# Attention with a squared-ReLU MLP: tiles on multiples of 128 bytes, another order of kinds in a pair's second half, and four small steps one step later

## The chip, the cores and the metric

One core of one Trainium2 chip. The metric is the device time of one execution in microseconds; a kernel is timed in several runs and the median is taken. Engines: TensorE (PE in the rows, its weight loads PEld), VectorE (DVE), ScalarE (ACT), GpSimd (POOL), and SyncE (SP), which issues nearly all DMAs here.

## The reference

```
q_pool = q.reshape(B, H, S//2, 2, D).mean(axis=3)      # B=4, H=8, S=1152, D=64: 576 pooled queries
scores = q_pool @ k^T / sqrt(D);  scores -= max(scores)
attn = exp(scores);  attn /= sum(attn) + 1e-9
x = (attn @ v) laid out as 2304 tokens x 512
out = (s * relu(x @ w_in)**2 + b) @ w_out               # 512 -> 2048 -> 512
```

## The kernel before

The program has two stages. Attention runs over 32 heads, two by two: 16 pairs. The MLP follows in three sweeps over 9 token blocks of 256, with features 0 to 2, 3 to 8 and 9 to 15 of 16.

**Attention, step by step.** A head's 1152 keys are 9 blocks of 128, and a step `n` does one block, so a pair has 18 steps, here called step 0 to 17 of the pair (n % 18). In step `n` TensorE computes the scores of block `n` (tile `s`, four matmuls, L497), one or two maximum units for a later pair (tile `m`, L465, each followed by a reduction into `pm` on VectorE), and the value products of block `n - 3` (tile `o`). The order of these parts within a step is the table `ORD`. The order of every other engine's instructions is that in which the code is written: `later(k, f)` puts `f` at the end of the k-th step counted from the present one, and the tables `PREP`, `VS` and `XT` say at which step of a pair a preparation is issued. No scheduler moves anything after that.

**Kinds.** The scores of a block are exponentiated in one of three ways, by the table `KIND` with 18 letters:

- `w`: ScalarE writes one float32 tile `pe`; the value product is four float32 matmuls (L529).
- `v`: ScalarE writes the rounded `ph`, then the full value back into PSUM over `s`; VectorE writes the remainder `pl` = `s` - `ph` (L512); the value product is six matmuls (L535, L537, L539). `s` is free only when `pl` is written.
- `g`: as `v`, but the full value goes to `pe` and GpSimd writes `pl`.

There are two `s` tiles. The scores of step n therefore wait for whatever frees the `s` tile of step n - 2: ScalarE for `w` and `g`, VectorE's `pl` for `v`. `pl(12)` below is the remainder of step 12.

**What else stands in a pair's steps.** `ka`, `kb` and `qt` transpose the next keys and queries on VectorE (`kT`, `kT`, `qT`); `qh`, `qz`, `kl`, `ql` and the roundings `kh` run on GpSimd, `qm` on ScalarE. `prep_v` rounds the next head's values on GpSimd (`vv`, and `vl` behind it at the step's end), from `vf`, which SyncE is told to load four steps earlier. When a head's last value product is done (`finish`), ScalarE copies it to `xu`, VectorE transposes the sums (`invert`, tile `lt`), takes reciprocals and spreads them (`rr`), and GpSimd scales (`xo`). `XT` holds the five delays of these. The first of them puts `invert` at the end of step 11 for head one of a pair, and at the end of the next pair's step 2 for head two.

**Where tiles lie.** The pools put tiles one behind the other in each partition, in order of the code. `sb`, of 8 bytes, stands ahead of nearly all of them, `guard` (8 bytes) ahead of `kraw`, `c` (20 bytes) ahead of `vf`. In the built program the first sweep's weights, `xr` and `x` begin 32 bytes past a multiple of 128, and so do `kraw`, `qraw`, `kT`, `qT`, `kh` and `qh`; `vf`, `vv`, `vl`, `pe`, `ph` and `pl` begin 96 bytes past one; `kk`, `qq`, `qz`, `gh`, `gl`, the raw weights and the later sweeps' weights begin at multiples of 256.

Of the kernel before, what the change touches and what calls it, by code (L numbers as in the profile page):

```python
# [8 lines left out]
F32 = mybir.dt.float32  # L9
F32R = mybir.dt.float32r  # L10
# [21 lines left out]
KB = 384  # L32


KIND = "wvwvgvwvg" + "vwgvvwvgw"

PP = (("ka", 0), ("kb", 0), ("ha", 0), ("hb", 1), ("qs", 1), ("qt", 1), ("qm", 2), ("qh", 2), ("qz", 2), ("kl", 2), ("ql", 3), ("l0", 7))
PREP = (("qs", 9), ("ka", 10), ("kb", 11), ("ha", 11), ("qt", 12), ("hb", 12), ("kl", 12), ("qm", 13), ("qh", 13), ("qz", 13), ("ql", 14), ("l0", 4), ("l1", 13))
LR = 14
LD = 1  # L40
VS = (7, 16)
XT = (1, 2, 3, 4, 8)
SW = (3, 9)
CB, CP = 270, 18
WB = (7, 11)
# [7 lines left out]
def f32(ap):  # L53
    return ap.bitcast(F32)
# [3 lines left out]
def attention_moe_kernel(ctx: ExitStack, tc: tile.TileContext, q, k, v, w_in, w_out, s_in, b_in, out):  # L58
# [6 lines left out]
    P = 128  # L65
    NJ = S // P
    NB = S // 32
    NBQ = SQ // 32
    NT4 = SQ // P
# [10 lines left out]
    consts = ctx.enter_context(tc.tile_pool(name="consts", bufs=1))  # L80
# [2 lines left out]
    mox = ctx.enter_context(tc.tile_pool(name="mox", bufs=1))  # L83
    ep = ctx.enter_context(tc.tile_pool(name="ep", bufs=1))

    sb = consts.tile([P, 2], F32, name="sb")
    xd = [dram.tile([NC, P, SQ], F32, name=f"xd{b}") for b in range(B)]
    parts = {}
    ready = {}
# [131 lines left out]
    def later(k, fn):  # L221
        step[1] += 1
        queue.append((step[0] + k, step[1], fn))
# [97 lines left out]
    ap = att.enter_context(tc.tile_pool(name="ap", bufs=1))  # L321
# [8 lines left out]
    qm = ap.tile([P, P], F32R, name="qm")  # L330
# [2 lines left out]
    vfs = [late.tile([P, NJ, P], F32, name=f"vf{i}") for i in range(2)]  # L333
    vvs = [late.tile([P, NJ, P], F32R, name=f"vv{i}") for i in range(2)]
    vls = [late.tile([P, NJ, D if i == 0 else P], F32R, name=f"vl{i}") for i in range(2)]
    guard = ap.tile([P, 2], F32, name="guard")

    def side(hd, of="v"):

        h = hd % 2 if of == "v" else 1 - hd % 2  # L340
        return slice(h * D, (h + 1) * D)
# [17 lines left out]
    def load_q(p):  # L359
        qraw[p] = ap.tile([P, NBQ, 2, 32], F32, tag="qraw", name=f"qraw{p}")  # L360
        for r, b, h, c in quarters(p):
            for e in range(2):

                eng = nc.sync if p or (r.start == P - 32) else nc.scalar
                eng.dma_start(qraw[p][r, :, e], q[b, h, e::2, c].rearrange("(j t) i -> t j i", t=32))
# [3 lines left out]
    def load_v(hd):  # L369
        nc.sync.dma_start(vfs[hd % 2][:, :, side(hd)], v[hd // H, hd % H].rearrange("(j p) d -> p j d", p=P))  # L370
# [62 lines left out]
    def prep_v(hd):  # L433
        vf, vv, vl = vfs[hd % 2][:, :, side(hd)], vvs[hd % 2][:, :, side(hd)], vls[hd % 2]
        if hd % 2:
            vl = vl[:, :, side(hd)]
        hi_of(nc.gpsimd, vv, vf)

        def lo():
            nc.gpsimd.tensor_tensor(out=vl, in0=vf, in1=f32(vv), op=ALU.subtract)  # L440
            holds["v", hd % 2] = hd

        later(1, lo)
# [27 lines left out]
    def shift(hd, pm, full, rest):  # L471


        c = ap.tile([P, NT4 + 1], F32R, tag="c", bufs=2, name=f"c{hd}")
        row = qqs[hd % 3][:, 1].rearrange("p a n -> p (a n)")
        h = hd % 2
        nc.vector.tensor_reduce(out=c, in_=pm, axis=AX.X, op=ALU.max)

        eng = nc.scalar if hd < 3 else nc.sync

        def send():
            eng.dma_start(f32(row[D:D + 1, :NT4 * P]), f32(c[:, full]))
            eng.dma_start(f32(row[D:D + 1, NT4 * P:]), f32(c[h * D:(h + 1) * D, rest:rest + 1]))
            holds["c", hd % 3] = hd

        later(1, send)
# [4 lines left out]
    def score_step(hd, j, kind):  # L491
        assert holds["k", hd % 3] == holds["c", hd % 3] == hd
        kk, qq = kks[hd % 3], qqs[hd % 3]
        ps = ps_s.tile([P, 2, 512], F32, tag="s", name=f"s{hd}_{j}")
        for a in range(2):
            for i in range(2):
                nc.tensor.matmul(ps[:, a, :HALF], kk[:, i, j * P:(j + 1) * P], qq[:, i, a], start=(i == 0), stop=(i == 1))  # L497
        if kind != "v":
            pe = late.tile([P, 2, HALF], F32, tag="pe", bufs=PE, name=f"pe{hd}_{j}")
        if kind == "w":  # L500
            nc.scalar.activation(pe, ps[:, :, :HALF], AF.Exp, scale=SCALE)
            prob[hd, j] = pe, None
            return
        ph = late.tile([P, 2, HALF], F32R, tag="ph", bufs=PB, name=f"ph{hd}_{j}")
        pl = late.tile([P, 2, HALF], F32R, tag="pl", bufs=PB, name=f"pl{hd}_{j}")
        nc.scalar.activation(ph, ps[:, :, :HALF], AF.Exp, scale=SCALE)  # L506

        full = ps[:, :, :HALF] if kind == "v" else pe
        nc.scalar.activation(full, ps[:, :, :HALF], AF.Exp, scale=SCALE)  # L509
        prob[hd, j] = ph, pl  # L510
        eng = nc.vector if kind == "v" else nc.gpsimd
        fresh.append(lambda: eng.tensor_tensor(out=pl, in0=full, in1=f32(ph), op=ALU.subtract))  # L512
# [3 lines left out]
    inv = {}  # L516
# [27 lines left out]
    def finish(hd, a):  # L544
        p, h = divmod(hd, 2)
        if a == 0:
            xu[hd] = ep.tile([P, 2, HALF], F32, tag=f"xu{h}", name=f"xu{hd}")
        nc.scalar.activation(xu[hd][:, a], acc[hd][a][:, :HALF], AF.Identity, bias=guard[:, h:h + 1])
        if a == 0:
            return  # L550
        acc.pop(hd)
        x = xu[hd].rearrange("p a n -> p (a n)")

        def invert():
            if h == 0:
                inv[p] = ep.tile([P, NBQ, 32], F32, tag="lt", name=f"lt{p}")
            nc.vector.transpose(out=inv[p][side(hd)], in_=x[side(hd, "l")])  # L557

        def reciprocal():
            lt = inv[p]  # L560
            rc = inv[p] = ep.tile([P, NBQ, 1], F32, tag="rc", name=f"rc{p}")
            nc.vector.reciprocal(rc, lt[:, :, 0:1])

        def spread():
            rc = inv[p]
            inv[p] = ep.tile([P, NBQ, 32], F32, tag="lt", name=f"rr{p}")
            nc.vector.transpose(out=inv[p], in_=rc.to_broadcast([P, NBQ, 32]))

        def scale():
            xo = xs[p] = ep.tile([P, SQ], F32, tag="xo", name=f"xo{p}")  # L570
            rr = inv.pop(p).rearrange("p j c -> p (j c)")
            for i in (hd - 1, hd):
                r = side(i)
                nc.gpsimd.tensor_tensor(out=xo[r], in0=xu.pop(i)[r].rearrange("p a n -> p (a n)"), in1=rr[r], op=ALU.mult)

        def send():
            nc.sync.dma_start(xd[hd // H][(hd % H) // 2], xs.pop(p))

        if h == 0:
            later(XT[0], invert)  # L580
        else:
            for at, fn in zip(XT, (invert, reciprocal, spread, scale, send)):
                later(at, fn)
# [53 lines left out]
    for n in range(NS + LAG):  # L637
        hd, j = divmod(n, NJ)
# [4 lines left out]
        for part in ORD[at] if at is not None else "sff":  # L643
            if part == "s" and n < NS:
                score_step(hd, j, KIND[n % 18])
            elif part == "f":
# [10 lines left out]
        if n < NS:  # L657
            p, h = divmod(hd, 2)
# [3 lines left out]
            if n == LD:  # L662
                load_k(2)
                load_q(2)
            if n % 18 == PREP[0][1]:
                lays = {k: prep[k] for k in ("l0", "l1") if k in prep}
                prep = prep_pair(p + 2) if p + 2 < NPAIR else {}
            for name, at in PREP:

                ops = prep if name not in ("l0", "l1") or at < PREP[0][1] else lays  # L670
                if n % 18 == at and name in ops and n >= 8:
# [5 lines left out]
            if hd + 1 < NH:  # L677
                if j == LAG and hd >= 1:
                    load_v(hd + 1)
                if n % 18 in VS:  # L680
                    prep_v(hd + 1)
# [36 lines left out]
    for m in range(len(work) + DEPTH):  # L718
        if m < len(work):
            i, blk, f, fs = work[m]  # L720
# [10 lines left out]
        if m >= DEPTH:  # L731
            _, blk, f, fs = work[m - DEPTH]
# [35 lines left out]
```

## Time and profile before

| | us |
|---|---|
| median of 3 runs | 957.25 (955.07 to 959.66) |
| the profiled execution's own time | 954.59 |
| its span, first to last instruction | 952.8 |
| attention's steps, first score to last score | 24.4 to 533.4 |
| an ordinary pair | 30.9 to 31.0 |

The profiled execution lies 2.66 below the median of the runs, and 1.8 of its time is outside the span. In the profile's rows a time stands in us from the span's start; "idle before <- X" is how long the engine had nothing to do before an instruction and what ended that. A matmul's row begins when it starts to stream and its end is modelled, so that rows of TensorE overlap by some 0.15 us, and the first of the matmuls behind a float32 one shows some 0.2 us early. Ends of whole groups are compared for that reason.

### The profile page before, as it was taken

The numbers are of one execution on the slowest core, as the hardware profiler recorded it, in microseconds if no ns is written. First come the engines' busy times: TensorE is split into PE (matmuls) and PEld (weight loads), VectorE is DVE, ScalarE is ACT, GpSimd is POOL, SyncE is SP. The second block draws the span as 40 slices with busy tenths as digits, with TensorE's granted clock in tenths as the row PEclk, the third lists the DMA queues.
The fourth block names the chain that finished last, engine by engine and source line by source line (L and its number), as shares of the span: only waits on it lengthen the run. The fifth ranks groups of instructions, "written<-read, shape, count | busy, mean of one in ns | idle before, by whom it ended". The sixth has DMA issues, their size and how long they took to land.

```text
span 952.8 us, 16142 instructions
## 1 busy us (share of the span) xinstructions
PE 910.5 (96%) x5712; PEld 818.7 (86%) x5712; DVE 639.7 (67%) x1184; ACT 525.3 (55%) x990; POOL 530.1 (56%) x426
## 2 busy tenths in 40 slices
PE   3799999999999999999999999999999999999998
PEld 2688998889898888888888878889999899999997
DVE  4777777787778778988886477766667653333333
ACT  2566666666666666766677556654444343333332
POOL 6567676867686668778867577754544521111110
PEclk9799999999999999999999999999999999999999
DMA  9888989798977998897754155654354332223211
GB/s 146 135 158 159 157 157 148 148 147 168 140 161 144 186 144 167 157 185 140 172 140 104 60 165 197 220 189 156 111 165 146 133 111 67 75 82 111 67 45 45
DMA packets 255313, 131.18 MB, mean 138 GB/s; under 512 B 203776, under 2 KB 227328, under 8 KB 255232
## 3 DMA queue, kind: packets, MB, share of 16 engines
q1 hardware_dynamic: 251008, 129.69, 61.7%
q10 hardware_dynamic: 4224, 0.45, 0.5%
q8 instruction: 46, 0.75, 0.3%
q14 instruction: 35, 0.29, 0.1%
HBM read 68.68 MB, written 18.87 MB: 92 GB/s over the span
## 4 chain that ended last, share of the span: by engine, by line
PE 68%; DVE 11%; DMA 5%; POOL 5%; ACT 3%; issue 3%; SPq 2%; ACTq 0%; POOLq 0%; DVEq 0%
PE h L272 17%; PE y L299 17%; PE s L497 11%; PE o L529 6%; PE m L465 6%; PE o L539 4%; PE o L535 4%; PE o L537 4%; DVE pm L466 3%; DVE pl L512 2%; POOL pl L512 1%; DVE lt L557 1%; DVE kT L420 1%; DMA yd_True<-yo_True_False 1%; DMA xr<-xd 1%
## 5 line engine op out<-in xcount | busy, mean ns | idle before, releaser
L466 DVE TENSOR_REDUCE pm<-m 128x1 f32<-128x384 f32 x432 | 227.1, 546 | 77.6 <-PE m L465 76.3
L497 PE MATMUL s<-qq,kk 128*128 128x288 f32 x1152 | 222.4, 315 | 10.5 <-DVE pl L512 9.3
L272 PE MATMUL h<-x,wih 128*128 128x256 f32 x1152 | 213.6, 283 | 4.3 <-DVE gl L286 3.5
L497 PEld LDWEIGHTS s<-qq,kk 128*128 128x128 f32 x1152 | 174.7, 190 | 32.8 <-PE m L465 17.4
L272 PEld LDWEIGHTS h<-x,wih 128*128 128x128 f32 x1152 | 185.8, 189 | 19.7 <-DVE gl L286 4.7
L506 ACT ACTIVATE ph<-s 128x576 fp32r<-128x576 f32 x192 | 125.2, 652 | 75.9 <-PE s L497 72.2
L272 PE MATMUL h<-x,wil 128*128 128x256 f32 x576 | 162.2, 282 | 0.0
L512 POOL TENSOR_TENSOR pl<-pe,ph 128x576 fp32r<-128x576 f32 x64 | 91.4, 1427 | 107.8 <-ACT pe L509 101.4
L280 DVE SCALAR_TENSOR_TENSOR h<-h,sb,r 128x256 f32<-128x256 f32 x144 | 70.3, 488 | 114.9 <-ACT r L289 114.9
L253 POOL TENSOR_TENSOR x<-xr,x 128x1024 fp32r<-128x1024 f32 x27 | 65.1, 2410 | 146.3 <-ACT x L212 140.6
L465 PE MATMUL m<-kh,qz 128*128 128x384 f32 x384 | 142.7, 383 | 1.5 <-DVE pm L466 0.9
L529 PE MATMUL o<-pe,vf 128*128 128x288 f32 x384 | 119.4, 408 | 0.0
L539 PE MATMUL o<-pl,vv 128*128 128x288 f32 x384 | 113.8, 296 | 4.6 <-POOL pl L512 4.6
L289 ACT ACTIVATE r<-h 128x256 f32<-128x256 f32 x144 | 55.7, 387 | 111.8 <-PE h L272 111.7
L512 DVE TENSOR_TENSOR pl<-s,ph 128x576 fp32r<-128x576 f32 x128 | 96.2, 751 | 27.3 <-ACT s L509 25.4
L535 PE MATMUL o<-ph,vv 128*128 128x288 f32 x384 | 114.2, 297 | 0.0
L537 PE MATMUL o<-ph,vl 128*64 128x288 f32 (+1 forms) x384 | 113.3, 295 | 0.0
L299 PE MATMUL y<-wol,gh 128*128 128x512 f32 x288 | 113.1, 393 | 0.0
L299 PE MATMUL y<-woh,gl 128*128 128x512 f32 x288 | 113.0, 392 | 0.0
L299 PE MATMUL y<-woh,gh 128*128 128x512 f32 x288 | 112.7, 391 | 0.0
L272 PEld LDWEIGHTS h<-x,wil 128*128 128x128 f32 x576 | 109.6, 190 | 0.0
L283 ACT ACTIVATE gh<-h,sb 128x256 fp32r<-128x256 f32 x144 | 68.4, 475 | 64.5 <-DVE h L280 64.0
(91 smaller groups left out, 1528.0 us busy)
## 6 DMA issues: line engine op xcount, KB each, us to landing
kk<-kh SPq DMA_DIRECT2D x32, 576.0 KB, 6.3
kraw<-in_k_dram SPq DMA_DIRECT2D x64, 144.0 KB, 4.4
vf<-in_v_dram SPq DMA_DIRECT2D x32, 288.0 KB, 4.3
kk<-kT SPq DMA_DIRECT2D x32, 288.0 KB, 3.9
qq<-qh SPq DMA_DIRECT2D x64, 144.0 KB, 5.6
xr<-xd SPq DMA_DIRECT2D x18, 512.0 KB, 3.9
qraw<-in_q_dram SPq DMA_DIRECT2D x122, 72.0 KB, 3.7
wsti<-in_moe_w_in_dram SPq DMA_DIRECT2D x16, 512.0 KB, 4.5
```

The source lines that it names most:

```text
L272: nc.tensor.matmul(h[:, :TB], st[:, c, :], mv[:, c, :], start=(n == 0), stop=(n == 3 * NC - 1))
L280: nc.vector.scalar_tensor_tensor(out=t, in0=h[:, :TB], scalar=sb[:, 0:1], in1=r, op0=ALU.mult, op1=ALU.mult)
L299: nc.tensor.matmul(y[:, :DM], st[:, ts_], mv, start=(first and n == 0), stop=(last and n == 2))
L465: nc.tensor.matmul(ps[:, :KB], st, khs[p][:, e * KB:(e + 1) * KB], start=True, stop=True)
L466: nc.vector.tensor_reduce(out=pms[p][:, col, e:e + 1], in_=ps[:, :KB], axis=AX.X, op=ALU.max)
L497: nc.tensor.matmul(ps[:, a, :HALF], kk[:, i, j * P:(j + 1) * P], qq[:, i, a], start=(i == 0), stop=(i == 1))
L506: nc.scalar.activation(ph, ps[:, :, :HALF], AF.Exp, scale=SCALE)
L512: fresh.append(lambda: eng.tensor_tensor(out=pl, in0=full, in1=f32(ph), op=ALU.subtract))
L529: nc.tensor.matmul(o[:, :HALF], vfs[hd % 2][:, j], ph[:, a], start=first, stop=last)
L535: nc.tensor.matmul(o[:, :HALF], vv[:, j], ph[:, a], start=first, stop=False)
L537: nc.tensor.matmul(o[0:vl.shape[2], :HALF], vl[:, j], ph[:, a], start=False, stop=False)
L539: nc.tensor.matmul(o[:, :HALF], vv[:, j], pl[:, a], start=False, stop=last)
```

## The change

The sizes of three small tiles become 128 bytes, and `guard` moves into `sb`. No instruction is added or removed. In the built program `sb` still begins at a multiple of 128, and now every tile behind it does too: the first sweep's weights, `xr`, `x` and `xu` at multiples of 256; `kraw`, `qraw`, `kT`, `qT`, `kh`, `qh`, `kk`, `qq`, `qz`, `vf`, `vv`, `vl`, `pe`, `ph`, `pl`, `gh`, `gl`, the raw weights and the later sweeps' weights 128 bytes past one.

```
-KIND = "wvwvgvwvg" + "vwgvvwvgw"
+KIND = "wvwvgvwvg" + "vwgvwvwgv"
-PREP = (("qs", 9), ("ka", 10), ("kb", 11), ("ha", 11), ("qt", 12), ("hb", 12), ("kl", 12), ("qm", 13), ("qh", 13), ("qz", 13), ("ql", 14), ("l0", 4), ("l1", 13))
+PREP = (("qs", 9), ("ka", 10), ("kb", 11), ("ha", 11), ("hb", 12), ("kl", 12), ("qt", 13), ("qm", 14), ("qh", 14), ("qz", 14), ("ql", 15), ("l0", 4), ("l1", 13))
-VS = (7, 16)
-XT = (1, 2, 3, 4, 8)
+VS = (8, 17)
+XT = (2, 2, 3, 4, 8)
...
-    sb = consts.tile([P, 2], F32, name="sb")
+    sb = consts.tile([P, 32], F32, name="sb")
+    guard = sb[:, 2:4]
...
-    guard = ap.tile([P, 2], F32, name="guard")
...
-        c = ap.tile([P, NT4 + 1], F32R, tag="c", bufs=2, name=f"c{hd}")
+        c = ap.tile([P, 32], F32R, tag="c", bufs=2, name=f"c{hd}")[:, :NT4 + 1]
...
-            rc = inv[p] = ep.tile([P, NBQ, 1], F32, tag="rc", name=f"rc{p}")
+            rc = inv[p] = ep.tile([P, 32], F32, tag="rc", name=f"rc{p}")[:, :NBQ].unsqueeze(2)
```

The kinds of steps 9 to 17 were v w g v v w v g w and are v w g v w v w g v: four `v`, three `w` and two `g` in both. Step 13 turns from `v` to `w`, 14 from `w` to `v`, 15 from `v` to `w`, 17 from `w` to `v`.

VectorE, steps 12 to 14 of an ordinary pair, before. `m_13` to `m_17` are the maximum units, `pl_3` is the remainder of step 12 and `pl_4` that of step 13 (a head's blocks count from 0, so step 12 is block 3 of head two):

```order
L557 STREAM_TRANSPOSE lt_2989<-xu_2967 64x576
L466 TENSOR_REDUCE pm_2799<-m_13_3000 128x1
L466 TENSOR_REDUCE pm_2799<-m_14_3006 128x1
L477 TENSOR_REDUCE c_3009<-pm_2799 128x5
L512 TENSOR_TENSOR pl_3_2997<-s_3_2991,ph_3_2996 128x576
L422 STREAM_TRANSPOSE qT_2938<-qs_2939 128x576
L466 TENSOR_REDUCE pm_2799<-m_15_3033 128x1
L512 TENSOR_TENSOR pl_4_3029<-s_4_3023,ph_4_3028 128x576
L466 TENSOR_REDUCE pm_2799<-m_16_3056 128x1
L466 TENSOR_REDUCE pm_2799<-m_17_3062 128x1
```

The same place of VectorE in the changed kernel, down to the remainder of step 14 (`pl_5`):

```order
L466 TENSOR_REDUCE pm_2797<-m_13_2997 128x1
L466 TENSOR_REDUCE pm_2797<-m_14_3003 128x1
L477 TENSOR_REDUCE c_3006<-pm_2797 128x5
L512 TENSOR_TENSOR pl_3_2994<-s_3_2988,ph_3_2993 128x576
L557 STREAM_TRANSPOSE lt_3017<-xu_2966 64x576
L466 TENSOR_REDUCE pm_2797<-m_15_3029 128x1
L422 STREAM_TRANSPOSE qT_2937<-qs_2938 128x576
L466 TENSOR_REDUCE pm_2797<-m_16_3049 128x1
L466 TENSOR_REDUCE pm_2797<-m_17_3055 128x1
L512 TENSOR_TENSOR pl_5_3045<-s_5_3039,ph_5_3044 128x576
```

The transposition `lt` stood ahead of step 12's remainder and stands behind it; `qT` stands one reduction later; the remainder of step 13 is gone and that of step 14 comes after both transpositions and three reductions.

GpSimd, steps 4 to 11 of the same pair, before (`pl_4` and `pl_8` are head one's remainders of steps 4 and 8, `pl_2` that of step 11):

```order
L512 TENSOR_TENSOR pl_4_2818<-pe_4_2816,ph_4_2817 128x576
L574 TENSOR_TENSOR xo_2856<-xu_2558,rr_2839 64x576
L574 TENSOR_TENSOR xo_2856<-xu_2768,rr_2839 64x576
L214 TENSOR_SCALAR vv_106<-vf_104 128x9x64
L440 TENSOR_TENSOR vl_108<-vf_104,vv_106 128x9x64
L512 TENSOR_TENSOR pl_8_2906<-pe_8_2904,ph_8_2905 128x576
L419 TENSOR_TENSOR qs_2939<-qraw_2664 128x576
L512 TENSOR_TENSOR pl_2_2980<-pe_2_2978,ph_2_2979 128x576
```

The same place in the changed kernel:

```order
L512 TENSOR_TENSOR pl_4_2817<-pe_4_2815,ph_4_2816 128x576
L574 TENSOR_TENSOR xo_2855<-xu_2557,rr_2838 64x576
L574 TENSOR_TENSOR xo_2855<-xu_2765,rr_2838 64x576
L512 TENSOR_TENSOR pl_8_2903<-pe_8_2901,ph_8_2902 128x576
L215 TENSOR_SCALAR vv_106<-vf_104 128x9x64
L440 TENSOR_TENSOR vl_108<-vf_104,vv_106 128x9x64
L419 TENSOR_TENSOR qs_2938<-qraw_2662 128x576
L512 TENSOR_TENSOR pl_2_2979<-pe_2_2977,ph_2_2978 128x576
```

The remainder of step 8 no longer stands behind the rounding of the next head's values. From step 9 on GpSimd's order is the same in both kernels, and SyncE's order of DMAs is the same throughout.

## Rows read from the trace of the kernel before

**Rows 1.** The page, section 1: busy us, share of the span, instructions.
```profile
PE 910.5 (96%) x5712; PEld 818.7 (86%) x5712; DVE 639.7 (67%) x1184; ACT 525.3 (55%) x990; POOL 530.1 (56%) x426
```
**Rows 2.** Waits of TensorE and its weight loads, 60 to 533 (us, times, longest).
```profile
PE s L497 <- DVE pl L512: 7.0, 15, 0.5
PE o L539 <- POOL pl L512: 4.6, 4, 1.7
...
PEld o L539 <- POOL pl L512: 6.1, 5, 2.0
```
**Rows 3.** TensorE's order of time, scores of steps 13 to 17 and the next 0.
```profile
211.17 0.70 PE L497 MATMUL s<-qq,kk 128*128 128x288 f32 x4
...
213.59 0.77 PE L497 MATMUL s<-qq,kk 128*128 128x288 f32 x4 [0.49 <-DVE pl L512]
...
215.41 0.79 PE L497 MATMUL s<-qq,kk 128*128 128x288 f32 x4
...
217.01 0.69 PE L497 MATMUL s<-qq,kk 128*128 128x288 f32 x4
...
218.69 0.69 PE L497 MATMUL s<-qq,kk 128*128 128x288 f32 x4
...
220.15 0.90 PE L497 MATMUL s<-qq,kk 128*128 128x288 f32 x4
```
**Rows 4.** VectorE's order of time in steps 12 to 14 of that pair.
```profile
210.89 0.77 DVE L557 STREAM_TRANSPOSE lt<-xu 64x576 f32<-64x576 f32 x1
211.59 0.98 DVE L466 TENSOR_REDUCE pm<-m 128x1 f32<-128x384 f32 x2
...
212.69 0.75 DVE L512 TENSOR_TENSOR pl<-s,ph 128x576 fp32r<-128x576 f32 x1
213.36 0.77 DVE L422 STREAM_TRANSPOSE qT<-qs 128x576 f32<-128x576 f32 x1
214.05 0.52 DVE L466 TENSOR_REDUCE pm<-m 128x1 f32<-128x384 f32 x1
214.49 0.74 DVE L512 TENSOR_TENSOR pl<-s,ph 128x576 fp32r<-128x576 f32 x1
```
**Rows 5.** ScalarE there: step 12's second exponential.
```profile
211.12 0.67 ACT L509 ACTIVATE s<-s 128x576 f32<-128x576 f32 x1
```
**Rows 6.** GpSimd's order of time in steps 7 and 8 of the second pair.
```profile
79.59 0.68 POOL L214 TENSOR_SCALAR vv<-vf 128x576 fp32r<-128x576 f32 x1 [3.53 <-DMA vf<-in_v_dram]
80.35 1.44 POOL L440 TENSOR_TENSOR vl<-vf,vv 128x576 fp32r<-128x576 f32 x1
81.74 1.40 POOL L512 TENSOR_TENSOR pl<-pe,ph 128x576 fp32r<-128x576 f32 x1
```
**Rows 7.** ScalarE and TensorE in the second pair: step 8's exponential, step 10's products.
```profile
77.64 0.64 ACT L509 ACTIVATE pe<-s 128x576 f32<-128x576 f32 x1
...
81.49 0.29 PE L537 MATMUL o<-ph,vl 128*64 128x288 f32 x1
83.20 0.40 PE L539 MATMUL o<-pl,vv 128*128 128x288 f32 x1 [1.42 <-POOL pl L512]
```
**Rows 8.** GpSimd's order of time in the pair of rows 3: remainders of steps 11 and 16.
```profile
210.78 1.43 POOL L512 TENSOR_TENSOR pl<-pe,ph 128x576 fp32r<-128x576 f32 x1 [3.05 <-ACT pe L509]
...
220.60 1.43 POOL L512 TENSOR_TENSOR pl<-pe,ph 128x576 fp32r<-128x576 f32 x1
```
**Rows 9.** DMA issues (KB each, median us to landing), and VectorE's first wait.
```profile
xr<-xd SPq DMA_DIRECT2D x18, 512.0 KB, 3.9
wsti<-in_moe_w_in_dram SPq DMA_DIRECT2D x16, 512.0 KB, 4.5
...
DVE kT L418 <- DMA kraw<-in_k_dram: 10.4, 1, 10.4
```
**Rows 10.** Groups of TensorE in sweep one (540 to 613), then two (690 to 763).
```profile
L299 PE MATMUL y<-wol,gh 128*128 128x512 f32 x44 | 17.4, 395 | 0.0
...
L299 PE MATMUL y<-wol,gh 128*128 128x512 f32 x52 | 20.4, 392 | 0.0
```

## The prediction

> **What bounds the kernel now.** First the busy times: TensorE has work for 96% of the span, the next engine for 67% [rows 1]. Faster work elsewhere therefore pays only where TensorE stands still for it. Next the waits of TensorE and of its weight loads during attention's steady part [rows 2]: two recur. The scores wait for VectorE's remainder `pl`, and a value product waits for GpSimd's remainder. No DMA stands there. Since rows of TensorE overlap, the idle times understate what is lost, so I went on to the order of time.
>
> The first wait in an ordinary pair [rows 3]: the scores of step 14 start at 213.59, behind `pl`. Taking ends of the four matmuls, step 13 lasts from 211.87 to 214.36, 2.49 us. Step 17 does the same work (one score, one maximum unit, four float32 products) from 219.38 to 221.05, 1.67 us. So 0.82 us is lost. Step 14 lasts from 214.36 to 216.20, 1.84 us, against 1.68 us for step 16 with the same work (217.70 to 219.38): another 0.16. Step 15, of 1.50, loses nothing that I can see. The pair loses 0.98.
>
> Who is late there is read from VectorE [rows 4]. The scores of step 14 need the `s` tile of step 12, which `pl(12)` frees at 212.69 + 0.75 = 213.44; they start 0.15 later. `pl(12)` could have begun when ScalarE had written its input, at 211.12 + 0.67 = 211.79 [rows 5]. It stood behind `lt` and two reductions, and VectorE worked without a gap.
>
> The second wait belongs to few pairs. In the second pair the remainder of step 8 had its input at 77.64 + 0.64 = 78.28 [rows 7], but GpSimd does it at 81.74, behind `vv` and `vl`, and `vv` had waited 3.53 us for the DMA of `vf` [rows 6]. TensorE's next product starts at 83.20 where 81.49 + 0.13 was due, 0.13 being the distance of such matmuls (four in 0.69, the last of them 0.29 long: 0.40 / 3 [rows 3, 7]): 1.58 us lost.
>
> **The kinds and the transpositions.** Nothing is added, so each term is a wait that shortens, moves or appears. `lt` behind `pl(12)` takes 211.59 - 210.89 = 0.70 us off the way to it: `pl(12)` begins at 211.99, still after its input, and ends at 212.74. The scores of step 14 can then start at 212.89. Without a wait they would start at 211.17 + 1.67 = 212.84. Of 0.82 about 0.05 is left. Step 14's own 0.16 was the scores of step 15 waiting for the `s` tile of step 13, which `pl(13)` frees at 214.49 + 0.74 = 215.23 [rows 4], 0.18 ahead of them. Step 13 is now a `w`, and ScalarE frees its tile without VectorE. That loss goes too.
>
> What is late next is `pl(14)`, which did not exist. From the start of `pl(12)`, with the distances from start to start in [rows 4]: `pl` 0.67, `lt` 0.70, one reduction 0.44, `qT` 0.69, two reductions 0.98, so `pl(14)` begins at 211.99 + 3.48 = 215.47, ends at 216.22, and frees step 16's scores at 216.37. TensorE would want them at 212.89 + 1.68 + 1.50 = 216.07. A new wait of 0.30 arises, and the second matmul of such a group lags by 0.08 (0.77 against 0.69 for the four [rows 3]): 0.38. So a pair gains 0.98 - 0.05 - 0.38 = 0.55. The last two pairs hold no `qT` and no such wait, which leaves 14: 14 x 0.55 = 7.7 us. Bounds: nothing, if the new wait is as long as the old one; 14 x 0.98 = 13.7, if `pl(14)` is never late.
>
> Three moves are costed at nothing. Steps 15 to 0 exchange kinds, but the work of TensorE over the pair is the same. `pl(17)` has the whole of step 0, with a float32 product, ahead of the scores that need it; without that cover it would cost what `pl(14)` costs. `qT` one step later feeds `qh`, `qz` and `ql`, which stand behind `kh` and `kl` in GpSimd's order, and those two cover it; if GpSimd were through with them, `qh` would start up to 0.69 later, a place in VectorE's order. The reciprocals one step earlier against the transposition meet the same spreading step.
>
> **The rounding of values.** `vv` and `vl` behind the remainder of step 8 take the DMA's lateness out of its way. In the second pair that remainder could run from 78.28 to 79.7; `vv` has its data at 79.59 [rows 6] and then waits for nothing. Of this sort there are five: four seen as idle matmuls, 4.6 us, and five as idle weight loads, 6.1 us [rows 2]. The one read above is 1.42 us of idle matmul for 1.58 lost, so the four are 4.6 x 1.58 / 1.42 = 5.1. I take 5.5, between that and 6.1. Bounds: 1.6, the one case that I traced to the end, and 6.1. What is queued behind `vv` now: `vl`, `qs` and step 11's remainder. GpSimd sat idle 3.05 us ahead of that remainder [rows 8]; `vv` and `vl` need 81.74 - 79.59 = 2.15 of it [rows 6]. It is hidden, with 0.90 to spare.
>
> **The tiles' addresses.** The trace of before holds both cases. `xr`, 32 bytes past a multiple of 128, lands in 3.9 us, the raw weights of equal size, at multiples of 256, in 4.5 [rows 9]: no sign that the shifted tile costs time. TensorE's streaming of `wol` takes 395 ns in sweep one, where weights lie 32 past, and 392 in sweep two, where they lie at multiples of 256 [rows 10]; other work differs between the sweeps as well. I take nothing. Bounds: 0.7% (3 of 392) of TensorE's 910 us, 6.4 us, gained if any multiple of 128 is good; and 0.7% of the 340 us behind sweep one (613 to the span's end), 2.4 us, lost if only multiples of 256 are.
>
> The Trainium skill, DMA: Bandwidth & Descriptors, section How a descriptor splits into AXI transactions, says that a transfer is cut at 256-byte addresses and that one that starts between them pays for the bytes below its start. By this rule a piece of 128 bytes at 32 past costs 5 or 9 beats in turn, and in the changed kernel 4 or 8, an estimate of one seventh less; `xr`'s rows of 1024 bytes would cost 37 against 32, which the trace does not show [rows 9]. By the rule the sum would fall by a further 1.4 us, the seventh of the first load's 10.4, and the sum here goes without it.
>
> **The sum.** 7.7 + 5.5 = 13.2 us. Against the profiled execution's 954.59 that gives 941.4; the median of the runs lies 2.66 higher, so 944.
>
> **The rivals.** One, *the wait only moves*: VectorE has the same work in steps 9 to 16, and `pl(14)` has three reductions and two transpositions between it and `pl(12)`. If they run late by another half microsecond, step 16 loses what step 14 lost. Then the second wait's 5.5 alone remain: 952. For it: VectorE without a gap in [rows 4]. Against it: step 15 gives the chain 1.50 us more.
>
> Two, *aligned tiles are read faster*: the bound of 6.4 us from TensorE's streams comes on top, 944 - 6.4 = 938. For it: 395 against 392 [rows 10]. Against it: `xr` against the raw weights [rows 9].
>
> Three, *slower*: GpSimd's chain becomes the bound. From step 9 on it runs `qs`, step 11's remainder, `kh`, `kl`, `qh`, `qz`, `ql`, and then step 16's remainder, which ends at 222.03 [rows 8]; the value product that needs it comes at about 222.4 in the changed kernel (step 16 at 216.37; steps 16 and 0 of 1.67 + 0.18 = 1.85 us each, the 0.18 of a second maximum unit being 1.68 - 1.50; step 17 of 1.50; and an estimated 0.8 into step 1, the scores' 0.69 [rows 3] and a product). The spare is 0.90 + 0.4 = 1.3 us. If `vv` finds its data later than that after step 8's remainder, every further microsecond is lost once a pair. It decides against the change from 13.2 / 15 = 0.9 us a pair on; at 2.5 us late, 1.2 a pair, 944 + 18 = 962. Against it: in the late pair of [rows 6] the data came before the remainder would have ended.
>
> Four, *nothing happens*: the moved waits turn up elsewhere in full, 957.
>
> **Numbers.** A chance of 0.60 for the forecast, 0.14 for the first rival, 0.14 for the second, 0.06 for the third, 0.06 for the fourth. A measurement of this kernel tells about 0.5%, 4.8 us, from no change. The forecast and the second rival are faster by more, and the first lies just beyond the bound, half of it inside: faster 0.81, same 0.13, slower 0.06. The forecast's own range is 938 (`pl(14)` never late, 6.0 less) to 948 (one case of the second wait alone, 3.9 more). To leave out no more than 2 in 10 the range goes on to 933, where the second rival comes on top of most of that, and to 952, the first rival.
>
> **What would show it.** Right: the scores of step 14 start within 0.1 us of the last product, step 16's carry a wait of about 0.3 on `pl`, TensorE's waits on GpSimd's `pl` are gone from the list, and ordinary pairs last about 30.4 us. The addresses are shown by the first landing of `kraw` and by the 395 and 392. Wrong: a wait of 0.8 at step 16, GpSimd's `vv` waiting behind step 8's remainder, or MLP groups whose mean moves by more than 3 ns.

## The result, and the profile after

The changed kernel takes 942.06 us (median of 4 runs, 941.79 to 944.12) against 957.16 for the kernel before beside it: a ratio of 0.9851 (95% interval 0.9828 to 0.9873). The profiled execution took 941.79, its span is 940.0 us.

The span is 12.8 us shorter, where the forecast's sum was 13.2; by the medians the gain is 15.1, the profiled execution of the kernel before being a quick one. The gain is made up otherwise than forecast, though. The stages of the two traces:

| | before | after | |
|---|---|---|---|
| first scores | 24.4 | 22.0 | -2.4 |
| first to last scores | 509.0 | 494.0 | -15.0 |
| last scores to the span's end | 419.4 | 424.0 | +4.6 |
| an ordinary pair | 30.9 to 31.0 | 30.0 to 30.1 | -0.95 |
| an MLP item, sweeps two and three | 2.80 | 2.84 | +0.04 |

(An item is one feature of one token block: twelve products of `h` and six of `y`; sweeps two and three hold 9 x 13 = 117 items, and 117 x 0.04 = 4.7.)

TensorE's waits in attention's steady part, after (us in all, times, longest), to be held against [rows 2]:

```profile
PE s L497 <- DVE pl L512: 1.7, 2, 1.5
PE m L465 <- DVE pm L466: 1.1, 5, 0.4
PE s L497 <- DMA qq<-qT: 0.3, 1, 0.3
```

The value products' waits on GpSimd's `pl` are gone, and the scores' wait on VectorE's `pl` is left in two places instead of fifteen. TensorE's scores of steps 12 to 17 of an ordinary pair, in order of time, which answer to [rows 3]:

```profile
201.77 0.69 PE L497 MATMUL s<-qq,kk 128*128 128x288 f32 x4
203.52 0.70 PE L497 MATMUL s<-qq,kk 128*128 128x288 f32 x4
205.00 0.91 PE L497 MATMUL s<-qq,kk 128*128 128x288 f32 x4
206.89 0.70 PE L497 MATMUL s<-qq,kk 128*128 128x288 f32 x4
208.47 0.72 PE L497 MATMUL s<-qq,kk 128*128 128x288 f32 x4
210.35 0.69 PE L497 MATMUL s<-qq,kk 128*128 128x288 f32 x4
```

VectorE there, which answers to [rows 4]; the last row is the new remainder `pl(14)`:

```profile
204.24 0.75 DVE L512 TENSOR_TENSOR pl<-s,ph 128x576 fp32r<-128x576 f32 x1
205.02 0.77 DVE L557 STREAM_TRANSPOSE lt<-xu 64x576 f32<-64x576 f32 x1
205.72 0.51 DVE L466 TENSOR_REDUCE pm<-m 128x1 f32<-128x384 f32 x1
206.26 0.78 DVE L422 STREAM_TRANSPOSE qT<-qs 128x576 f32<-128x576 f32 x1
206.97 0.98 DVE L466 TENSOR_REDUCE pm<-m 128x1 f32<-128x384 f32 x2
207.87 0.74 DVE L512 TENSOR_TENSOR pl<-s,ph 128x576 fp32r<-128x576 f32 x1
```

No idle time of the matmuls stands ahead of these scores. The forecast gave step 16 a new wait, on `pl(14)`. Yet its scores start at 208.47, and `pl(14)` ends only at 207.87 + 0.74 = 208.61: it cannot be what they wait for. The built program says why. The two `s` tiles do not take turns: in the changed kernel step 14 has the tile of step 13, step 15 that of 12, step 16 that of 15 and step 17 that of 14. (Before, step 14 has that of step 12, but step 15 that of 14.) So step 16 follows a `w`, which ScalarE frees. Its exponential, and the weight loads of step 16 right behind it:

```profile
207.69 0.65 ACT L501 ACTIVATE pe<-s 128x576 f32<-128x576 f32 x1
208.40 0.56 PEld L497 LDWEIGHTS s<-qq,kk 128*128 128x128 f32 x4
```

This costs a little: by ends of the four matmuls step 15 lasts from 207.59 to 209.19, 1.60 us, where the step 15 of before took 1.50. The same rows of before explain its 0.16 at step 14, which the forecast put down to `pl(13)`. Step 15 took step 14's tile there, and its weights load 0.05 behind that step's exponential, not behind `pl(13)`, which had ended at 215.23:

```profile
214.71 0.65 ACT L501 ACTIVATE pe<-s 128x576 f32<-128x576 f32 x1
215.41 0.56 PEld L497 LDWEIGHTS s<-qq,kk 128*128 128x128 f32 x4
```

The start, in the DMA issues (KB each, median us to landing) and VectorE's first wait, against [rows 9]:

```profile
kraw<-in_k_dram SPq DMA_DIRECT2D x64, 144.0 KB, 3.3
qraw<-in_q_dram SPq DMA_DIRECT2D x122, 72.0 KB, 2.5
...
DVE kT L418 <- DMA kraw<-in_k_dram: 8.0, 1, 8.0
```

The raw keys and queries came in 4.4 and 3.7 us before; the first wait falls from 10.4 to 8.0. Both come in packets of 128 bytes, which in the first 12 us took 19.1 ns on average and now take 12.9. The MLP, a group of TensorE in sweep two of before (690 to 763) that [rows 10] left out, then the groups of after (670 to 745):

```profile
L299 PE MATMUL y<-woh,gh 128*128 128x512 f32 x52 | 20.3, 391 | 0.0
...
L300 PE MATMUL y<-woh,gh 128*128 128x512 f32 x53 | 21.1, 398 | 0.0
L300 PE MATMUL y<-wol,gh 128*128 128x512 f32 x52 | 20.5, 395 | 0.0
L300 PE MATMUL y<-woh,gl 128*128 128x512 f32 x52 | 20.5, 395 | 0.0
```

### The profile page after: what moved, and what is told of

Read it like the earlier page. It is cut to its first block, busy times and chain, and to the rows that moved or that the text cites. A ratio compares the mean times of both kernels' runs of the same rounds, so it can differ in the third digit from the quotient of the medians.

```text
span 940.0 us, 16065 instructions
## 1 busy us (share of the span) xinstructions
PE 910.0 (97%) x5712; PEld 824.6 (88%) x5712; DVE 642.4 (68%) x1184; ACT 525.1 (56%) x990; POOL 530.7 (56%) x426
## 4 chain that ended last, share of the span: by engine, by line
PE 84%; DVE 7%; POOL 2%; DMA 2%; ACT 2%; issue 1%; SPq 0%; DVEq 0%; ACTq 0%; POOLq 0%
PE h L273 20%; PE y L300 19%; PE s L497 15%; PE o L529 8%; PE m L465 8%; PE o L537 5%; PE o L539 5%; PE o L535 5%; DVE pm L466 2%; DMA wsto<-in_moe_w_out_dram 1%; DVE pl L512 1%; DVE wabo L162 1%; POOL pl L512 0%; DMA xr<-xd 0%; DVE lt L557 0%
## 5 line engine op out<-in xcount | busy, mean ns | idle before, releaser
L497 PE MATMUL s<-qq,kk 128*128 128x288 f32 x1152 | 217.3, 311 | 4.4 <-DVE pl L512 2.8
L465 PE MATMUL m<-kh,qz 128*128 128x384 f32 x384 | 155.4, 421 | 1.9 <-DVE pm L466 1.8
L529 PE MATMUL o<-pe,vf 128*128 128x288 f32 x384 | 121.7, 407 | 0.0
```

The lines of the kernel that those rows point to most:

```text
L465: nc.tensor.matmul(ps[:, :KB], st, khs[p][:, e * KB:(e + 1) * KB], start=True, stop=True)
L529: nc.tensor.matmul(o[:, :HALF], vfs[hd % 2][:, j], ph[:, a], start=first, stop=last)
```

## Experiments

Theory: the tables alone make attention's 15 us; the tiles' places make the start earlier and the MLP slower, two effects that work against each other. Main rival: the forecast, by which places do nothing. All medians come with 95% intervals of their ratio to the kernel before.

**Tiles alone and tables alone.** e1_tiles has the diff's four tile lines only, e2_tables the four table lines only.

> The tiles of the changed kernel with the tables (kinds, preparations, roundings, reciprocals) of before. Theory A, the forecast's own: addresses move nothing, so 957, as before. Theory B, from the two traces: the order of steps alone gives the whole of attention's gain, and the addresses shift two other stages against each other, the first scores from 24.4 to 22.0 us and an MLP item of sweeps two and three from 2.80 to 2.84 us. B expects 957.2 - 2.4 + 4.5 = 959, ordinary pairs of 30.9 to 31.0 us, first scores at 22.0 and MLP items of 2.84 us. Theory C: aligned tiles quicken attention itself too (the pair is 0.95 shorter where I had forecast 0.55, so 0.4 a pair, 6 us, may be theirs): pairs of 30.5 and 953.

> The tables of the changed kernel with the tiles of before. Theory A (addresses move nothing): 942, as the changed kernel. Theory B: the whole gain of attention, 15 us, without the earlier start and without the slower MLP: 957.2 - 15 = 942, made up of first scores at 24.4, pairs of 30.05, MLP items of 2.80 us. A and B part in the stages, not in the sum. Theory C (tiles give 0.4 a pair): pairs of 30.45, 948.

| | median | ratio | first scores | ordinary pair | item |
|---|---|---|---|---|---|
| e1_tiles | 956.22 | 1.0003 (0.9991 to 1.0015) | 22.2 | 30.93 | 2.84 |
| e2_tables | 942.44 | 0.9857 (0.9840 to 0.9874) | 24.2 | 30.10 | 2.80 |

All the gain is the tables'. By the sum, A was nearer: the kernel before took 956.04 beside e1, so that A asked for 956 and B for 958, which lies outside the interval. The stages, each read from one profiled execution, are B's: e1 has the early start, the old pairs and the slow items, e2 the late start, the short pairs and the quick items. So A falls as a mechanism: places do move two stages. But by the stages they should cost 2.2 us in all, and neither e1's median (0.2 above before) nor e2's ratio beside the changed kernel's (0.9857 and 0.9851) shows that cost; what makes up the rest stays open. C falls too: with the changed tables, aligned tiles shorten an ordinary pair by 0.05 (30.10 to 30.05), not by 0.4.

**The values' rounding.**

```
-VS = (8, 17)
+VS = (7, 16)
```

> The changed kernel with the values' rounding back at steps 7 and 16. The forecast priced this part at 5.5 us (bounds 1.6 and 6.1). If that holds: 947.5, with TensorE's waits on GpSimd's pl back in four or five pairs, of 0.3 to 2 us. Rival: with the other order of kinds the load of vf comes early enough, or the pair has slack to take it, so that the waits are not back: 942 to 943.

947.06 us, ratio 0.9903 (0.9887 to 0.9918): 5.0 above the changed kernel; in the two profiles attention's steps are 3.9 longer (497.9 against 494.0). Its waits in attention's steady part:

```profile
PE o L539 <- POOL pl L512: 4.8, 4, 2.7
...
PE m L465 <- DVE pm L466: 1.1, 5, 0.4
PE s L497 <- DMA qq<-c: 0.6, 1, 0.6
```

Four waits on GpSimd's `pl` are back, the rival falls, and the term of 5.5 is right within what can be measured.

**The kinds without the moves, the moves without the kinds.** In e5_kind `KIND` is that of before; in e6_lt `PREP` and `XT` are.

```
-KIND = "wvwvgvwvg" + "vwgvwvwgv"        # e5_kind
+KIND = "wvwvgvwvg" + "vwgvvwvgw"
...
-... ("qt", 13), ("qm", 14), ("qh", 14), ("qz", 14), ("ql", 15) ...   # e6_lt
+... ("qt", 12), ("qm", 13), ("qh", 13), ("qz", 13), ("ql", 14) ...
-XT = (2, 2, 3, 4, 8)
+XT = (1, 2, 3, 4, 8)
```

> The changed kernel with before's letters in KIND; preparations, roundings, reciprocals and tiles stay changed. Theory A (the forecast's: two s tiles in turn, so that the scores of step 14 wait for pl(12), which the move of lt and qT frees 0.7 us earlier): the move alone keeps 0.77 of a pair's 0.98, pairs of about 30.2, 944. Theory B (the built order of the s tiles decides: in this kernel step 14 again takes step 12's tile, and pl(12) is early since lt stands behind it): the same 30.1 to 30.2, 943 to 945. If the kinds were needed for the gain, pairs stay at 30.9 and the time at 942 + 12 = 954.

> The changed kernel with before's PREP and XT, so that lt stands ahead of the remainder of step 12 again and qT behind it at once; kinds, roundings and tiles stay changed. Theory A (the forecast's: the scores of step 14 wait for pl(12)): the loss of 0.7 us a pair at step 14 is back, 14 x 0.7 = 10, so 952. Theory B (in the changed kernel step 14 takes the s tile of step 13, a w that ScalarE frees, so lt ahead of pl(12) stands in nobody's way): pairs of 30.05 to 30.1, 942 to 943.

e5_kind: 950.16, ratio 0.9931 (0.9906 to 0.9956), pairs of 30.7. e6_lt: 951.51, ratio 0.9956 (0.9941 to 0.9972), pairs of 30.65. Both theories missed e5 by 5 to 7 us. On e6 the number is A's, but not for A's reason: the scores of step 14 start there while `pl(12)` is still running (207.36 to 208.11). In neither kernel does the scores' old loss come back; a maximum unit waits instead. VectorE of e5_kind, and the unit of step 15 on TensorE:

```profile
208.29 0.76 DVE L512 TENSOR_TENSOR pl<-s,ph 128x576 fp32r<-128x576 f32 x1
208.97 0.77 DVE L422 STREAM_TRANSPOSE qT<-qs 128x576 f32<-128x576 f32 x1
209.66 1.61 DVE L466 TENSOR_REDUCE pm<-m 128x1 f32<-128x384 f32 x3
...
210.23 0.44 PE L465 MATMUL m<-kh,qz 128*128 128x384 f32 x1 [0.48 <-DVE pm L466]
```

and of e6_lt, where it is the unit of step 14; the second row is step 14's scores, early beside `pl(12)`:

```profile
207.36 0.75 DVE L512 TENSOR_TENSOR pl<-s,ph 128x576 fp32r<-128x576 f32 x1
207.37 0.90 PE L497 MATMUL s<-qq,kk 128*128 128x288 f32 x4
208.02 0.77 DVE L422 STREAM_TRANSPOSE qT<-qs 128x576 f32<-128x576 f32 x1
208.72 1.62 DVE L466 TENSOR_REDUCE pm<-m 128x1 f32<-128x384 f32 x3
...
209.29 0.45 PE L465 MATMUL m<-kh,qz 128*128 128x384 f32 x1 [0.30 <-DVE pm L466]
```

The `m` tiles too are two. In both kernels a remainder and `qT` follow each other, three reductions pile up behind them, and the next unit finds no free tile (0.30 and 0.48 of idle matmul; in the order of time the step loses 0.56 and 0.75). With kinds and moves together a remainder and a transposition (`lt`) still stand ahead of a reduction, but a step earlier, where the unit is not late for it, and `qT` has reductions on both sides, as in the rows of after. The forecast's first rival, "the wait only moves", is what each half does alone, at another waiter than it named.

**The s tiles in strict turn.**

```
-ps_s = att.enter_context(tc.tile_pool(name="ps_s", bufs=2, space=PSUM))
+ps_s = att.enter_context(tc.tile_pool(name="ps_s", bufs=1, space=PSUM))
...
-        ps = ps_s.tile([P, 2, 512], F32, tag="s", name=f"s{hd}_{j}")
+        ps = ps_s.tile([P, 2, 512], F32, tag=f"s{(hd * 9 + j) % 2}", name=f"s{hd}_{j}")
```

> The changed kernel with its two s tiles made to alternate strictly, step by step; nothing else differs. In the built program of the changed kernel they don't: step 14 takes the tile of step 13, 15 that of 12, 16 that of 15, 17 that of 14. Theory A (the forecast's working is right for tiles that alternate, and only the built order spared the new wait): the scores of step 16 now wait for pl(14), which ends at 208.61 where they start at 208.47 in the trace of the changed kernel; with 0.15 behind it a wait of 0.29 and 0.08 of lag, 0.37 a pair, pairs of 30.4, 14 x 0.37 = 5.2, so 947. Theory B (the scores would not wait anyway, VectorE being earlier than I reckoned): pairs of 30.05, 942.

948.80, ratio 0.9912 (0.9897 to 0.9927), ordinary pairs of 30.37. VectorE's `pl(14)`, the scores of steps 15 to 17, and a row of the waits in attention's steady part:

```profile
213.03 0.70 PE L497 MATMUL s<-qq,kk 128*128 128x288 f32 x4
...
214.02 0.74 DVE L512 TENSOR_TENSOR pl<-s,ph 128x576 fp32r<-128x576 f32 x1
...
214.90 0.77 PE L497 MATMUL s<-qq,kk 128*128 128x288 f32 x4
216.83 0.69 PE L497 MATMUL s<-qq,kk 128*128 128x288 f32 x4
...
PEld s L497 <- issue: 4.6, 14, 0.3
```

Step 16 now starts 0.14 behind the end of `pl(14)` at 214.76, 1.87 behind step 15, where after has 208.47 - 206.89 = 1.58: 0.29, and the lag is in the 0.77. By ends, step 15 lasts from 213.73 to 215.67, 1.94 us. That is 0.34 more than in the changed kernel, whose pair is 0.32 shorter, and 0.44 more than the 1.50 from which the forecast reckoned its 0.38. This is the forecast's wait, in a kernel whose tiles take turns as the forecast assumed. The matmuls' own list hides it, since their rows overlap; that of the weight loads shows it, 14 times 0.3 us, 13 of them at step 16. The total has another part that I had not thought of: during the start the maximum units use the `s` tiles as well, here only one of them, and the first scores come at 26.3 instead of 22.0.

**Where the MLP's tiles lie.**

```
-... ep.tile([P, 32], F32, tag="rc" ...
+... ep.tile([P, 64], F32, tag="rc" ...        # e3_256;  [P, 256] in e9_rc1k;  [P, 24] in e11_x160
...
+    wb.tile([P, 32], F32, name="pad")         # e7_w0_g128 alone, ahead of the later sweeps' weights
...
+            mox.tile([P, 40], F32, name="pad") # e11_x160 alone, ahead of xr and x
```

> The changed kernel with the tile rc of 256 bytes instead of 128, so that all large tiles behind it begin at multiples of 256, among them the later sweeps' weights, gh and gl. Theory A: 942, nothing moves. Theory B: MLP items of sweeps two and three return from 2.84 to 2.80 us while the early start stays: 942 - 4.5 = 937.5, first scores at 22.0, pairs of 30.05. Rival: the MLP's 0.04 us an item comes from something else that the change moved (the end of attention, the order of its last loads), then 942 and items of 2.84.

> The changed kernel with 128 spare bytes ahead of the later sweeps' weights: these begin at multiples of 256, gh and gl stay 128 past one, as in the first sweep of the changed kernel, where the six products of y take 1.154 us (first to sixth) against 1.166 in sweep two, and h's twelve 1.315 against 1.318. If the pair of places of weights and gh decides, sweep two shows 1.154 too, an item of about 2.825, and the MLP 15 x 0.1 = 1.6 us less than the changed kernel. Rival: only gh and gl count, or the sweep's other work: 1.166 and 2.84.

> The changed kernel with the tile rc of 1024 bytes: the later sweeps' weights and gh, gl begin 256 past a multiple of 1024, where they lie before the change; with rc of 256 bytes they begin 512 past one, and an item of sweeps two and three takes 2.82 us, half-way between before (2.80) and the changed kernel (2.84). If the place within 1024 bytes decides: items of 2.80, the six y products at 1.147, span 937.4 - 2.3 = 935 and a median of about 939. Rival: the place within 256 bytes is all that counts for these tiles, and the other half is x's, which lies 160 past a multiple of 256 before and at one since: items of 2.82 again, y at 1.161, and 941.

> The changed kernel with 160 spare bytes ahead of xr and rc of 96 bytes: x lies 160 past a multiple of 256, as before the change, while the later sweeps' weights, gh, gl and the tiles of attention begin at multiples of 256 and the first sweep's weights too. With weights, gh and gl at multiples of 256 and x there as well, items of sweeps two and three took 2.82 us, whether 512 or 256 past a multiple of 1024. If x's place makes the other half: items of 2.80, y's six at 1.147, h's twelve at 1.306, span 937 - 2.3 = 935, median 938 to 939, the fastest of all. Rival: neither x nor these is the cause (the tile's absolute place, or sb's size): 2.82 and 941.

Sweep two in the traces (bytes past a multiple of 256; from first to last start of the products, medians in us):

| | later weights | gh, gl | x | 12 of h | 6 of y | item |
|---|---|---|---|---|---|---|
| before, e2_tables | 0 | 0 | 160 | 1.306 | 1.147 | 2.80 |
| after, e1_tiles | 128 | 128 | 0 | 1.318 | 1.166 | 2.84 |
| e7_w0_g128 | 0 | 128 | 0 | 1.312 | 1.154 | 2.82 |
| e3_256, e9_rc1k | 0 | 0 | 0 | 1.313 | 1.161 | 2.82 |
| e11_x160 | 0 | 0 | 160 | 1.307 | 1.148 | 2.80 |

e3_256: 941.33, ratio 0.9842 (0.9823 to 0.9861); B's 937.5 is a miss, since items came only half-way back. e9_rc1k: 940.39, 0.9827 (0.9802 to 0.9853): 256 or 512 past a multiple of 1024 makes no difference, the rival holds. e7_w0_g128: one run, 939.73, with `y` as expected. e11_x160: 938.40, ratio 0.9799 (0.9784 to 0.9814), items as before and first scores at 21.7; it is faster than both kernels. Its groups in sweep two:

```profile
L274 PE MATMUL h<-x,wih 128*128 128x256 f32 x212 | 39.3, 282 | 0.2 <-DVE gl L288 0.2
...
L301 PE MATMUL y<-wol,gh 128*128 128x512 f32 x54 | 21.2, 392 | 0.0
L301 PE MATMUL y<-woh,gl 128*128 128x512 f32 x54 | 21.1, 391 | 0.0
L301 PE MATMUL y<-woh,gh 128*128 128x512 f32 x54 | 21.1, 391 | 0.0
```

So the places of the weights and `gh` make half of the 0.04 us (in e7_w0_g128 the weights' alone did) and the 160 bytes ahead of `xr` the other half. These 160 bytes also move `xu` and `rc`. Of the tiles that they move TensorE reads only `x` in the MLP; but `y`, which does not read `x`, quickens as well, so that which tile it is stays open.

**64 bytes.** e8_64 has 64 spare bytes ahead of `kraw`.

```
+    ap.tile([P, 16], F32, name="pad")
```

> The changed kernel with 64 spare bytes ahead of kraw: kraw, qraw and what lies behind them begin 64 past a multiple of 128 (32 past one before the change, at one since). If pieces of 128 bytes are quick only when they begin at multiples of 128: kraw lands in about 4 us as before (4.4; 3.3 since), and first scores come at 24 us, 2 us more in all. If multiples of 64 are enough: 3.3 us, 22.0, no change. A piece at 32 past touches five stretches of 32 bytes and 64 past it four, so multiples of 64 may be cheaper or not; no row shows it yet.

One run of 944.92, first scores at 24.2:

```profile
kraw<-in_k_dram SPq DMA_DIRECT2D x64, 144.0 KB, 4.2
```

In this run multiples of 64 were not enough for pieces of 128 bytes. (The expectation counted wrongly: at 32 past, as at 64 past, such a piece touches four stretches of 32 bytes.)

## Why the prediction was right, and where it was not

The sign and the sum were right (13.2 against 12.8 of span, 15.1 by the medians). That the sum came so near to the span's is luck: attention gained 15.0 where the two terms had 13.2, and the start and the MLP, which it took as nothing, gave 2.2 back.

- *The wait at step 14 goes.* Right: 0.82 and 0.16 are gone from the pair. The step behind it, that step 14 waits for `pl(12)`, which the moved `lt` frees, was wrong for the changed kernel: step 14 takes step 13's tile. e6_lt has that tile too, and its scores start ahead of the end of `pl(12)`, with `lt` in its old place. The 0.16 was ScalarE's exponential and not `pl(13)`; a wait of its kind is back at step 16, for 0.10.
- *"What is late next is `pl(14)`", 0.38 a pair.* This is the step that failed. It rested on "the scores of step n wait for whatever frees the `s` tile of step n - 2", which I took from the code and did not look up in the built program. e10_alt shows the working to be right for tiles in turn. An ordinary pair gained 0.95 instead of 0.55, near the bound of 0.98. The term of 7.7 became 15.0 less the 6.0 us that before's late value products lose in the order of time, some 9.0 us; it is not 14 x 0.95 = 13.3, because the first pair got 0.6 longer, pairs 11 to 15 still take 1.0 to 1.3 more than an ordinary one, and the last two gain nothing.
- *Not seen at all:* the maximum units' wait for VectorE's reductions. In the changed kernel it is hidden, and it is the price of doing half of the change (e5_kind, e6_lt).
- *The rounding of values, 5.5.* Right: 5.0 by e4_vs (3.9 in its profile), and the waits left the list.
- *The addresses, nothing.* Wrong as a mechanism, nearly right as a sum. The start gained 2.4 us. I had compared `xr` with the raw weights, packets of 1024 bytes and more, and carried this over to `kraw`'s of 128. The MLP lost 4.6, where I had bounded a loss at 2.4 from one group (3 of 392 ns) and the time behind sweep one. The bound divided by the wrong length: rows of products overlap, and the six of `y` start every 1.147 / 5 = 0.229 us. There 3 ns is 1.3%, and 1.3% of the 340 us is 4.5. `woh,gh` moved from 391 to 398, more than the 3 ns that the forecast named as a sign of being wrong.
- The rule of the Trainium skill (DMA: Bandwidth & Descriptors, How a descriptor splits into AXI transactions) gave the start's gain with the right sign; the estimate from it was 1.4 (a seventh of 10.4 is 1.5), the trace shows 2.4. The rule speaks of bytes that are fetched; here it was carried over to where they are written. By the same rule pieces at 64 past would cost more than at 32 past (6 or 10 beats of 32 bytes in turn against 5 or 9), which e8_64 doesn't show: `kraw` lands in 4.2 against 4.4.
- *Rivals.* Aligned tiles being read faster (938) is refuted by e1_tiles. The chain of GpSimd (962) did not become the bound: TensorE's list has no wait for it.

## What to carry to other kernels

Before you chain a wait through a pool of buffers, read from the built program which buffer each tile got; "two buffers" need not mean "n waits for n - 2", and the difference was 0.32 us a pair here. When you free one waiter of a busy engine, look for every tile that this engine frees in the same steps, since the wait can go to the other one, and two moves may be worth nothing like the sum of each alone. Measure a change of addresses stage by stage: its gain in one stage can hide its loss in another. Where rows of one engine overlap, price a longer product by the distance between starts and not by the length of its row.

## What the hardware showed that I had not expected

- Landing in pieces of 128 bytes depends on where in SBUF they begin: 12.9 ns a packet on multiples of 128 (after), 19.1 at 32 past (before), 18.9 at 64 past (e8_64, one run), all in the crowded first 12 us.
- The pace of TensorE's products depends on where its operands lie, by up to 1.7% (six of `y` in 1.147 to 1.166 us), and not by alignment in a simple order: with weights and `x` at 0, `gh` at 128 is quicker (1.154, e7_w0_g128) than `gh` at 0 (1.161, e3_256), and the 160 bytes ahead of `xr` quicken `y`, which reads neither `x` nor `xr`. What in the chip does this stays open.
